# Delta-rule attention with an expert layer: key norms from the Gram diagonal, and a new order of the first four passes

## The chip, the cores and the metric

One core of a Trainium2 chip. The metric is the device time of one execution in microseconds (us): median of 3 runs, 619.43 before the change.

## What is computed

The reference is a linear attention with the delta rule, 32 heads (batch 4, 8 heads) of 768 steps and width 48, followed by a dense layer of two matrices with a softplus between.

```
k_n = k / (norm(k) + 1e-6)
for t in range(768):
    y[:, :, t] = q_t @ state
    v_old = k_t @ state
    state = state + beta_t * outer(k_t, v_t - v_old)
x = y.transpose(0, 2, 1, 3).reshape(3072, 384)
h = x @ w_in                                   # 384 -> 2048
out = (max(h, 0) + log1p(exp(-abs(h)))) @ w_out  # 2048 -> 384
```

## The kernel before

**Chunks, pairs, passes.** Time is cut into 12 chunks of 64 steps. Inside a chunk all heads are solved at once: the Gram products of the keys (L207 to L248) give a lower triangular system, whose 32-wide diagonal blocks are inverted for two chunks together. Such a pair is numbered u = 0 to 5. For pairs 0 and 1 (`N16`) the inversion goes to 16 x 16 blocks only, and `join_w`, `join_z`, `join_d` (L347 to L370) put two of them together by products. `cross_a`, `arrange` and `cross_b` (L374 to L407) then form the off-diagonal block of the inverse. For each chunk follow `k_state` (K times state), `v_less` (the subtraction from V), `p_all` and `mask_p` (Q times K, masked), `u_all` (inverse times V), `y_all` and `state` (the new state).

**One pass per chunk.** The rows of y of chunk m are input x of the dense layer, and pass m runs it in eight half-sets f0 = 0, 2 .. 14 of two hidden tiles each: `ph_mm` (L546 to L561, first matrix), `sp_act` (ScalarE: Abs, Exp, Ln), `sp_dve` (VectorE: the softplus, L573 or L577), and, two half-sets later, `out_mm` (second matrix). One `ph_mm` or one `out_mm` is called a half-step below. The attention of chunk m+1 and later is placed between them. Passes 0 and 1 use the weights as single 32-bit values; from pass 2 on weights and operands are split in two parts (`split`, L539 to L543), with three products each.

**The weights.** They are doubles, 16 tiles f = 0 to 15 of 0.79 MB. Each is loaded (L492), its magnitude taken on ScalarE (`mag`, L507) and converted on VectorE in four instructions (`weights`, L523, L526, L529, L534). A call `("fill", n)` issues n such instructions. Four tiles are loaded at the start; a later load f + 4 is held back by a small GpSimd copy (`hold`, L158) until tile f - 1 is converted.

**Norms and inversion.** `norms` (L256 to L294) loads K rows (`kN`), squares them on ScalarE (L261, L268), adds them up on VectorE (L270), takes the root by Ln and Exp with one Newton step (L275 to L282), and forms beta over the squared norm as column cT and its negative ncT (L286 to L293). `invert` (L296 to L338) selects a triangle of ncT on GpSimd (L302), transposes the Gram blocks on VectorE (L307), multiplies the two (L311, L313) and runs 14 steps of two instructions on each of two blocks (pairs 0 and 1) or 30 steps on the whole (L331, L337). `finish` (L340 to L345) makes the two transposes of the result.

**What sets the order.** All engines run their instructions in the written order. It is written out by hand in tables of calls: `GRAMS` and `START` for all that comes before the first half-step, `FIRST` for pass 0, `PLAN` for the later passes (pass, half-step, call, argument), `INV` and `RATE` for how many steps of an inversion go at each of four places of a half-set, `CASTS` for the half-sets whose rounding is on ScalarE. `("warm", n, c)` issues n products of zeros with c columns on TensorE (L162). `("inv", n)` issues n steps of the inversion in work. DMAs are issued from SyncE's queue in an order of its own, in which a wait holds up all behind it; the copy of the last 16 columns of y into x (L482) goes by SyncE's and, in chunk 0, half by ScalarE's queue.

Before the first half-step the order is: K rows of chunks 0 and 1, kT of chunks 1 and 0, beta, q; norms of pair 0; Gram products; inversion of pair 0; join, cross and u of chunk 0; y of chunk 0. The norms of pair 1, its Grams and the join of chunk 1 stand between these, warm-up products too.

## Time and profile before

| | us |
|---|---|
| median of 3 runs | 619.43 |
| lowest and highest | 616.36, 620.22 |
| the profiled execution | 622.68 |
| its span in the profile | 621.0 |
| TensorE busy | 595.0 (96%) |
| VectorE busy | 449.4 (72%) |
| ScalarE busy | 369.8 (60%) |
| GpSimd busy | 32.8 (5%) |
| granted TensorE clock, mean | 0.973 of full speed |
| HBM read, written | 37.06 MB, 4.72 MB |

PE is TensorE, PEld its weight loads, DVE VectorE, ACT ScalarE, POOL GpSimd, SP SyncE, and SPq or ACTq a queue's DMA issues. A row in order of time gives start, duration, engine, line, operation, output and inputs by the program's names, shape and count; in brackets stands how long the engine was idle before and what released it. A group's row gives busy us, mean ns of one, then idle time. A line of waits gives the sum, the number and the longest. Warm-up products count as busy, so the share of TensorE alone does not tell what it could give up.

### The profile page before, as it was taken

The numbers are of one execution on the slowest core, as the hardware profiler recorded it, in microseconds if no ns is written. First come the engines' busy times: TensorE is split into PE (matmuls) and PEld (weight loads), VectorE is DVE, ScalarE is ACT, GpSimd is POOL, SyncE is SP. The second block draws the span as 40 slices with busy tenths as digits, with TensorE's granted clock in tenths as the row PEclk, the third lists the DMA queues.
The fourth block names the chain that finished last, engine by engine and source line by source line (L and its number), as shares of the span: only waits on it lengthen the run. The fifth ranks groups of instructions, "written<-read, shape, count | busy, mean of one in ns | idle before, by whom it ended". The sixth has DMA issues, their size and how long they took to land.

```text
span 621.0 us, 22953 instructions
## 1 busy us (share of the span) xinstructions
PE 595.0 (96%) x10196; PEld 541.8 (87%) x10196; DVE 449.4 (72%) x941; ACT 369.8 (60%) x743; POOL 32.8 (5%) x70
## 2 busy tenths in 40 slices
PE   7888897999999999999999999999999999999997
PEld 3856675777778999999999999998999999999997
DVE  4985899972799976789873988964998654354433
ACT  4332666436878678864568747558745645644443
POOL 5000110000100000000010000010000000000000
PEclk8777889999999999999999999999999999999999
DMA  9842573211132313202311212211203101100000
GB/s 207 302 153 86 158 269 144 60 58 55 30 64 60 92 30 104 50 18 83 91 58 47 61 43 69 74 33 53 65 2 88 32 26 39 29 29 14 20 6 27
DMA packets 34996, 45.42 MB, mean 73 GB/s; under 512 B 21585, under 2 KB 26897, under 8 KB 34897
## 3 DMA queue, kind: packets, MB, share of 16 engines
q1 hardware_dynamic: 34800, 43.91, 24.8%
q8 instruction: 80, 1.31, 0.9%
q14 instruction: 20, 0.16, 0.1%
q10 hardware_dynamic: 96, 0.05, 0.0%
HBM read 37.06 MB, written 4.72 MB: 67 GB/s over the span
## 4 chain that ended last, share of the span: by engine, by line
PE 77%; DVE 10%; ACT 7%; issue 3%; DMA 2%; ACTq 0%; SPq 0%; DVEq 0%
PE ph L559 30%; PE po L606 28%; PE pa L466 4%; PE po L162 3%; PE pa L451 2%; PE pa L413 2%; PE pa L425 2%; DVE w L543 1%; DMA kt<-kT 1%; PE pa L439 1%; PE pa L402 1%; DVE Z L337 1%; DVE work L331 1%; DVE ltq L307 1%; PE pa L379 1%
## 5 line engine op out<-in xcount | busy, mean ns | idle before, releaser
L559 PE MATMUL ph<-x,w 128*128 128x256 f32 x1452 | 211.4, 299 | 8.3 <-DVE w L534 2.8
L559 PEld LDWEIGHTS ph<-x,w 128*128 128x128 f32 x1452 | 195.6, 191 | 19.4 <-issue 4.5
L606 PE MATMUL po<-w,gh 128*128 128x384 f32 x688 | 191.4, 370 | 0.0
L565 ACT ACTIVATE a<-ph 128x512 f32<-128x512 f32 x96 | 57.4, 598 | 172.7 <-PE ph L559 169.9
L606 PEld LDWEIGHTS po<-w,gh 128*128 128x128 f32 x688 | 121.0, 188 | 15.3
L577 DVE SCALAR_TENSOR_TENSOR a<-ph,a 128x512 f32<-128x512 f32 x80 | 54.9, 686 | 70.4 <-ACT a L567 69.9
L606 PE MATMUL po<-w,gl 128*128 128x384 f32 x280 | 94.1, 336 | 0.0
L566 ACT ACTIVATE a<-a 128x512 f32<-128x512 f32 x96 | 60.7, 632 | 3.0
L567 ACT ACTIVATE a<-a 128x512 f32<-128x512 f32 x96 | 60.7, 632 | 3.0
L589 DVE TENSOR_TENSOR gl<-a,gh 128x512 fp32r<-128x512 f32 x80 | 55.4, 692 | 2.6
L606 PEld LDWEIGHTS po<-w,gl 128*128 128x128 f32 x280 | 52.6, 188 | 0.0
L337 DVE TENSOR_TENSOR Z<-Z,work 128x84 f32<-128x84 f32 (+14 forms) x148 | 44.3, 307 | 4.1
L331 DVE TENSOR_TENSOR work<-Z,ltq 128x84 f32<-128x84 f32 (+14 forms) x148 | 43.7, 303 | 2.2
L584 DVE CAST gh<-a 128x512 fp32r<-128x512 f32 x76 | 32.4, 426 | 2.5
L395 POOL MEMSET tt<- 32x512 f32 x24 | 12.4, 518 | 405.7 <-ACT tt L393 378.8
L432 DVE TENSOR_TENSOR big<-pa,maskP 64x512 f32<-64x512 f32 x44 | 30.2, 687 | 0.5
L466 PEld LDWEIGHTS pa<-big 128*64 128x64 f32 x768 | 25.0, 145 | 2.2 <-issue 1.1
L307 DVE STREAM_TRANSPOSE ltq<-work 128x1024 f32<-128x1024 f32 x6 | 12.9, 2154 | 19.4 <-ACT work L220 17.6
L466 PE MATMUL pa<-big 128*64 128x64 f32 x768 | 26.7, 231 | 0.0
L162 PE MATMUL po<-zero 128*128 128x128 f32 (+2 forms) x108 | 21.8, 364 | 2.0 <-issue 2.0
L559 PE MATMUL ph<-x,v 128*128 128x256 f32 x180 | 23.1, 282 | 0.0
L559 PEld LDWEIGHTS ph<-x,v 128*128 128x128 f32 x180 | 22.6, 189 | 0.0
(124 smaller groups left out, 718.4 us busy)
## 6 DMA issues: line engine op xcount, KB each, us to landing
w<-wts SPq DMA_DIRECT2D x16, 768.0 KB, 8.0
kt<-kT SPq DMA_DIRECT2D x12, 448.0 KB, 3.9
big<-qT SPq DMA_DIRECT2D x24, 192.0 KB, 4.4
nv<-vN SPq DMA_DIRECT2D x12, 384.0 KB, 3.4
ki<-kI SPq DMA_DIRECT2D x24, 192.0 KB, 3.4
out<-ex SPq DMA_DIRECT2D x24, 192.0 KB, 2.0
ka<-kN SPq DMA_DIRECT2D x8, 384.0 KB, 3.6
x<-x SPq DMA_DIRECT2D x60, 32.0 KB, 2.0
```

Source lines behind the costliest of these rows:

```text
L162: nc.tensor.matmul(to[:, 0:cols], zero, zero.unsqueeze(1).to_broadcast([P, cols // P, P]), start=True, stop=True)
L331: nc.vector.tensor_tensor(tmp[:, a:a + r, 0:j], Z[:, a + j + 1:a + n, a + j:a + j + 1].to_broadcast([P, r, j]), lq[:, a + j:a + j + 1, a:a ...
L337: nc.vector.tensor_tensor(z, z, tmp[:, a:a + r, 0:j], op=ALU.add)
L466: nc.tensor.matmul(py[tk[ab], i, :], big[:, at + C:at + 2 * C], big[:, at:at + C], start=True, stop=True)
L559: nc.tensor.matmul(ph[:, f - f0], weight(s, f, a, k * P, P), xr[b][k], start=(c == 0), stop=(c == len(terms) * NK - 1))
L565: nc.scalar.activation(a, PH[s, f0], AF.Abs)
L566: nc.scalar.activation(a, a, AF.Exp, scale=-1.0)
L567: nc.scalar.activation(a, a, AF.Ln, bias=1.0)
L577: nc.vector.scalar_tensor_tensor(a, ph, 0.0, a, op0=ALU.max, op1=ALU.add)
L584: nc.vector.tensor_copy(g[0], a)
L589: nc.vector.tensor_tensor(g[1], a, g[0], op=ALU.subtract)
L606: nc.tensor.matmul(po, g[b][:, f - f0, h * P:(h + 1) * P], weight(s, f, a, DM, DM), start=(f == 0 and i == 0), stop=end)
```

## The change

- Key norms: the Gram blocks hold the squared norms on their diagonal. `norms` reads them there, after the transpose of the Gram blocks, with a step of 33 elements (`lq`, now inside `invert`). `kN` is no longer passed or loaded, the squares and sums are gone, and beta comes already transposed, so cT needs no transpose; the norms for scaling V get one instead.
- Start: kT of chunks 1, 0 and 2 are the first DMAs. A one-element GpSimd copy that reads kT of chunk 0 stands ahead of the loads of q and beta. Four warm-up products instead of three. The four copies of the block below the diagonal of chunk 0 come after those that the inversion needs. `arrange` moves its copies ahead of `cross_a` in chunk 0.
- Loads of weight tiles 4 and 5 are gathered in a list and issued by `("later",)` at the end of `START`, on SyncE behind the copy of x.
- The Grams of pair 1 move from `START` to the sixth half-set of the first pass, and its inversion, with the norms, to the second pass. `join_w` of chunk 1 comes behind the first half-set.
- New tables for the first four passes: where `fin`, `join`, `ca`, `cross_b`, `us`, `ys`, `gs` stand, a row of `INV` (passes 1 to 3) and of `RATE` (later ones) for each half-set instead of one per pass, nine `CASTS` instead of four. The steady table loses its `nms` calls.

The diff, cut to its core:

```
-    ("load_k", 2), ("kas",), ("load_v", 0), ("iv0", 2), ("load_w", 2), ("hold", 0, "Z"), ("p_0",),
...
+    ("load_w", 1), ("load_v", 0), ("load_w", 2), ("load_w", 3), ("load_ki", 0), ("load_w", 0),
+    ("below_1",), ("iv0", 6), ("load_v", 1), ("p_0",), ("warm", 1, 512), ("below_0",), ("mag",),
+    ("masks_0",), ("iv0", 8), ("mag",), ("warm", 1, 256), ("warm", 7, 512), ("iv0", 97),
+    ("join_w", 0), ("join_z", 0), ("scale_v", 0), ("mask_p0", 0), ("join_d", 0), ("mask_p0", 1),
+    ("warm", 1, 256), ("ca", 0), ("cross_b", 0), ("fill", 2), ("warm", 1, 256), ("u_all", 0),
+    ("fill", 2), ("warm", 1, 128), ("y_all", 0), ("fill", 4), ("later",), ("warm", 2, 512),
...
 FIRST = {
+        ("join_w", 1), ("fill", 9), ("join_z", 1), ("state_0",), ("sp",), ("scale_v", 1),
+        ("join_d", 1), ("fill", 7),
...
+        ("fill", 20), ("inv", 2), ("gs", 2), ("out",), ("gs", 3), ("sp",),
...
-    def norms(u, kas=None):
+    def norms(u, ss):
...
+        nc.vector.tensor_scalar(sm, ss, 1e-30, None, op0=ALU.max)
...
+        nc.vector.tensor_tensor(cT, r0, bet[:, u], op=ALU.mult)
+        nc.vector.tensor_scalar(ncT, cT, -1.0, None, op0=ALU.mult)
+        nc.vector.transpose(nn, nt)
...
-    def invert(u, cT, ncT):
+    def invert(u):
...
+        nc.vector.transpose(lq.rearrange("p j i -> p i j"), LTD[u].rearrange("p q i -> p i q"))
+        yield
+        cT, ncT = yield from norms(u, lq.rearrange("p a b -> p (a b)")[:, 0:HB * HB:HB + 1])
...
+                if later is None:
                     hold(ST[f + AHEAD], ST[f - 1][:, 0:1].bitcast(F32))
-                load_weights(f + AHEAD)
+                    load_weights(f + AHEAD)
+                else:
+                    later.append(f + AHEAD)
...
-            nc.sync.dma_start(kas[0][0], kN[0])
-            nc.sync.dma_start(kas[0][1], kN[1])
             load_k(1)
             load_k(0)
...
+            warm(idle, 4)
...
+            nc.gpsimd.tensor_copy(bv[dr[0], 0, 0, 0:1], kts[0][dr[0], 0, 0:1])
+            load_q(0)
+            nc.sync.dma_start(bet, beta)
```

Three places show how instructions stand. In such a row: line, operation, output and inputs, shape, times in a row; line numbers are those of the kernel that is shown.

VectorE at the start of the inversion of pair 0, first before (ss and nn are sums and norms, ltq the transposed Gram blocks, Z the triangle):

```order
L282 TENSOR_SCALAR nn<-r_237 128x32
L286 TENSOR_TENSOR r_237<-nn 128x32
L287 RECIPROCAL r_237<-r_237 128x32
L288 TENSOR_TENSOR r_237<-r_237,bet 128x32
L292 STREAM_TRANSPOSE cT<-r_237 128x32
L293 TENSOR_SCALAR ncT<-cT 128x32
L254 COPY work<-po_128 32x8x32
L307 STREAM_TRANSPOSE ltq<-work 128x32x32
L311 TENSOR_TENSOR ltq<-ltq,Z 128x16x16
```

and with the change:

```order
L275 STREAM_TRANSPOSE ltq<-work 128x32x32
L250 TENSOR_SCALAR sm<-ltq 128x32
L256 RECIPROCAL r_252<-rt 128x32
L257 TENSOR_TENSOR r_252<-r_252,sm 128x32
L258 TENSOR_TENSOR r_252<-r_252,rt 128x32
L259 TENSOR_SCALAR nt<-r_252 128x32
L261 TENSOR_TENSOR r_252<-nt 128x32
L262 RECIPROCAL r_252<-r_252 128x32
L263 TENSOR_TENSOR cT<-r_252,bet 128x32
L264 TENSOR_SCALAR ncT<-cT 128x32
L265 STREAM_TRANSPOSE nn<-nt 128x32
L287 TENSOR_TENSOR ltq<-ltq,Z 128x16x16
```

The norms stood ahead of the transpose of the Gram blocks (L307 before, L275 now) and now stand between it and the first multiply.

TensorE from the join of chunk 0 to its y, first before (tt is the inverse, off the block below the diagonal, big the operands of y; po is written by warm-up products, L162 before and L152 now):

```order
L379 MATMUL pa<-tt,off 32x32 x32
L162 MATMUL po_311<-zero 128x128 x2
L162 MATMUL po_311<-zero 128x256
L162 MATMUL po_311<-zero 128x128
L402 MATMUL pa<-off,tt 32x32 x32
L162 MATMUL po_311<-zero 128x256
L439 MATMUL pa<-nv,tt 64x48 x32
L353 MATMUL pa<-tt,x_316 32x16 x64
L162 MATMUL po_311<-zero 128x128 x2
L466 MATMUL pa<-big 64x64 x32
```

and with the change, from the warm-up products ahead of the join on:

```order
L152 MATMUL po_310<-zero 128x512 x7
L329 MATMUL pa<-tt,x_323 32x16 x64
L339 MATMUL pa<-x_323,tt 32x16 x64
L152 MATMUL po_310<-zero 128x256
L357 MATMUL pa<-tt,off 32x32 x32
L381 MATMUL pa<-off,tt 32x32 x32
L152 MATMUL po_310<-zero 128x256
L418 MATMUL pa<-nv,tt 64x48 x32
L152 MATMUL po_310<-zero 128x128
L445 MATMUL pa<-big 64x64 x32
```

`join_w` of chunk 1 (L353 before) no longer stands between u (L439, now L418) and y (L466, now L445), and fewer warm-up products stand between the join and y.

VectorE in the first pass, first before, from the third weight tile on:

```order
L534 SCALAR_TENSOR_TENSOR w_92<-w_92,ex 128x768
L523 TENSOR_SCALAR ex<-ex 128x768
L307 STREAM_TRANSPOSE ltq<-work 128x32x32
L311 TENSOR_TENSOR ltq<-ltq,Z 128x16x16
L526 TENSOR_SCALAR ex<-ex 128x768
L529 SCALAR_TENSOR_TENSOR ex<-w_93,ex 128x768
```

and with the change, from the last weight tile on:

```order
L518 SCALAR_TENSOR_TENSOR ex<-w_1237,ex 128x768
L523 SCALAR_TENSOR_TENSOR w_1237<-w_1237,ex 128x768
L562 SCALAR_TENSOR_TENSOR gh<-ph,a 128x512 x3
L275 STREAM_TRANSPOSE ltq<-work 128x32x32
L250 TENSOR_SCALAR sm<-ltq 128x32
L562 SCALAR_TENSOR_TENSOR gh<-ph,a 128x512
```

The inversion of pair 1 began among the conversions of the first pass and now begins behind the last of them and three softplus.

More of the change, by code (lines that the diff above doesn't have):

```diff
@@ L508, in mag, with load_later @@
         exs.append(ex)
+    def load_later():
+        nonlocal later
+        for f in later:
+            load_weights(f)
+        later = None
     def weights():
@@ L625, in deltanet_moe @@
     done, conversion = [0], weights()
-    cols = {}
-    def ahead(s):
-        if s % 2 == 0 and 2 <= s < NS - 2:
-            return norms(s // 2 + 1)
-        return None
     def kp(s):
+        if s == 2:
+            scale_v(s)
         k_state(s)
@@ L671, in gs @@
         if s % 2:
-            while s // 2 not in cols:
-                nms(s // 2, 1)
             background.append(solve(s // 2))
     def solve(u):
-        for _ in range(WAIT):
+        for _ in range(WAIT if u > 2 else 0):
             yield
-        yield from invert(u, *cols[u])
-        if u < 3:
+        yield from invert(u)
+        if u < 2:
             finish(u)
```

189 lines of the change are left out of this document (63 added, 126 removed), and 6 rows, old and new, of the table PLAN.

## The prediction

> **What bounds the kernel now.** I read first the busy time by stage (columns: stretch, its length, then busy us and instructions of PE, PEld, DVE, ACT, POOL, granted clock, DMA share, GB/s), then the weight conversion (first and last start at the end), then, stage by stage, instructions in order of time (start, us, engine, line).
>
> ```profile
> 60.00:80.00 20.00, 16.27 (x537) 13.25 (x528) 16.94 (x24) 12.92 (x26) 3.12 (x8) 0.89 0.45 127
> 80.00:100.00 20.00, 19.28 (x133) 13.67 (x130) 18.94 (x27) 12.90 (x21) 2.59 (x8) 0.94 0.78 272
> 100.00:120.00 20.00, 16.27 (x234) 12.16 (x235) 19.44 (x41) 11.11 (x22) 0.00 (x0) 1.00 0.25 72
> 200.00:300.00 100.00, 99.58 (x1725) 96.33 (x1717) 82.63 (x174) 70.09 (x147) 3.34 (x5) 1.00 0.24 63
> ```
>
> ```profile
> L534 DVE SCALAR_TENSOR_TENSOR w<-w,ex x16: 939/958/967, 35.1 to 117.6; 128x768 int32<-128x768 int32 x16
> ```
>
> From 200 us on TensorE is busy 99.6% of the time: nothing is to be had there but its idle crumbs. From 60 to 120 us it lacks 8.2 us and VectorE is busy 55.3 of 60 us; the sixteenth weight tile is converted only at 118.5, and the first pass cannot end before. So the price of this change is decided by when VectorE finishes the sixteen tiles, which hangs on when the chain for chunk 0 lets it begin and what else it does meanwhile. I follow that in five stages. Sums are made in the profiled run (622.68 us, span 621.0) and carried to the median 619.43.
>
> **Stage A, to the inverse of pair 0.**
>
> ```profile
> 1.13 5.49 PE L162 MATMUL ph<-zero 128*128 128x512 f32 x6 [1.13 <-DVE zero L728]
> 8.73 1.16 PE L247 MATMUL po<-kt 48*64 48x64 f32 x64 [2.11 <-DMA kt<-kT]
> 11.46 1.84 PE L234 MATMUL pa<-kt 48*32 48x64 f32 x59
> ```
>
> ```profile
> 10.70 0.16 DVE L275 TENSOR_SCALAR rt<-ss 128x32 f32<-128x32 f32 x1
> 13.31 0.21 DVE L292 STREAM_TRANSPOSE cT<-r 128x32 f32<-128x32 f32 x1
> 13.56 0.18 DVE L293 TENSOR_SCALAR ncT<-cT 128x32 f32<-128x32 f32 x1
> 16.16 2.03 DVE L307 STREAM_TRANSPOSE ltq<-work 128x1024 f32<-128x1024 f32 x1 [1.74 <-ACT work L254]
> 18.30 0.42 DVE L311 TENSOR_TENSOR ltq<-ltq,Z 128x256 f32<-128x256 f32 x1
> 20.07 0.20 DVE L327 COPY Z<-cT 128x32 f32<-128x32 f32 x1
> 21.58 1.41 DVE L432 TENSOR_TENSOR big<-ph,maskP 64x512 f32<-64x512 f32 x2
> 28.45 2.00 DVE L343 STREAM_TRANSPOSE tt<-Z 128x1024 f32<-128x1024 f32 x1
> 30.31 1.92 DVE L344 STREAM_TRANSPOSE tt<-Z 128x1024 f32<-128x1024 f32 x1
> ```
>
> ```profile
> 13.81 0.96 POOL L302 TENSOR_SCALAR_AFFINE_SELECT Z<-ncT 128x256 f32<-128x256 f32 x2 [5.46 <-DVE ncT L293]
> ```
>
> The first Gram product waited for kT until 8.73; 0.79 MB of K rows had been issued ahead. Now kT goes first, but four warm-up products stand before it: 5.49/3 = 1.83 each, so TensorE is free at 1.13 + 7.3 = 8.45. I take kT as landed by then (bounds: as late as before, +1.0; early does not help). Gram of chunk 1 ends at 9.6, of chunk 0 after 2.72 us (the stretch from 10.58 to 13.30 before) at 12.3. One diagonal copy and one block copy of 0.43 follow on VectorE, since the four copies below the diagonal no longer stand ahead on ScalarE: the transpose starts at 13.3 instead of 16.16 and ends at 15.4.
>
> Before, the norms lay in front of it, so the first multiply came 0.1 us behind the transpose. Now they follow it: 10.70 to 13.74 is 3.04, less the 0.21 transpose, is 2.83; then half of the 0.96 on GpSimd and hops: first multiply at 19.0, the copy of the diagonal at 20.8 (before 20.07). This is the price of the diagonal: 3.5 us in the chain, of which 2.8 come back by the earlier start. The fourteen steps took 8.4 us with the 1.44 of a mask in between, which moves behind the transposes. They end at 27.7, the transposes (3.78) at 31.4, before 32.2. Gain only 0.8.
>
> ```profile
> 148.63 1.09 PE L234 MATMUL pa<-kt 48*32 48x64 f32 x62
> ```
>
> The second half of a later Gram, above, takes 1.09 us where chunk 0's took 1.84: TensorE ran faster there. A rule speaks to this. The Trainium skill, "TensorE: Matmul & The Clock Gate", section on the HAM clock gate, lets TensorE out of half speed after one busy window of about 3.4 us that runs free of the kernel. The trace agrees only if no whole window fell into the 5.49 busy us, since the products stayed slow; four fill 7.3 us, which holds one wherever it starts. By that rule chunk 0's Gram would take 1.6 us instead of 2.7 and the sum below would be 608.7. I stay with the slow rows.
>
> **Stage B, from the transposes to y of chunk 0.**
>
> ```profile
> 39.33 3.78 PE L162 MATMUL po<-zero 128*128 128x512 f32 x5 [2.01 <-issue]
> 43.04 1.08 PE L379 MATMUL pa<-tt,off 32*32 32x32 f32 x64
> 52.50 1.29 PE L353 MATMUL pa<-tt,x 32*32 32x16 f32 x81 [1.67 <-issue]
> 54.88 3.75 PE L466 MATMUL pa<-big 128*64 128x64 f32 x64
> 65.23 3.62 PE L559 MATMUL ph<-x,w 128*128 128x256 f32 x8 [1.92 <-DMA x<-x]
> ```
>
> ```profile
> 38.88 0.71 DVE L370 STREAM_TRANSPOSE tt<-tt 128x512 f32<-128x512 f32 x1
> ```
>
> Here lies the first large term. Before, VectorE converted nearly two tiles ahead of the join's second half, which ended at 39.6, 7.4 us behind the transposes, and TensorE was then still in warm-up products until 43.1. Now VectorE does scale_v (0.9), two of the four mask instructions (1.4) and the join's subtraction and transpose (1.2): it ends at 34.9, with one short warm-up on TensorE. Cross_a starts at 35.0 instead of 43.04: 8.0 earlier. Its copy of the block row now stands ahead of the evictions on ScalarE, 1.3 more; but join_w of chunk 1 is gone from between u and y. It took from 50.3 to 53.8, its idle 1.67 included, and the warm-ups behind it 1.2. So cross_a to y takes 11.84 - 4.6 + about 0.9 = 8.1: y starts at 43.1, 11.8 earlier. From there to the first product of the experts were 10.35 us; I leave them: 53.4. Unknown here: q is now issued only when kT of chunk 0 has landed, and nine warm-ups follow its product. Should they last past 32, join_w slips one for one; bounds 0 and +3.
>
> **Stage C, the first pass: VectorE's queue.**
>
> ```profile
> L529 DVE SCALAR_TENSOR_TENSOR ex<-w,ex 128x768 int32<-128x768 int32 x15 | 14.4, 957 | 0.4
> L534 DVE SCALAR_TENSOR_TENSOR w<-w,ex 128x768 int32<-128x768 int32 x15 | 14.3, 956 | 0.8
> L526 DVE TENSOR_SCALAR ex<-ex 128x768 int32<-128x768 int32 x16 | 9.3, 581 | 0.4
> L523 DVE TENSOR_SCALAR ex<-ex 128x768 f32<-128x768 f32 x16 | 8.8, 553 | 0.7 <-ACT ex L507 0.7
> L573 DVE SCALAR_TENSOR_TENSOR gh<-ph,a 128x512 f32<-128x512 f32 x6 | 4.1, 679 | 2.4 <-ACT a L567 2.4
> 58.66 0.56 DVE L471 COPY x<-pa 128x384 f32<-128x384 f32 x1 [5.69 <-PE pa L466]
> ```
>
> A tile costs 0.553 + 0.581 + 0.957 + 0.956 = 3.05 us. VectorE copies y until 59.5 - 11.8 = 47.7, with one tile done. To the sixteenth: 15 x 3.05 = 45.7, five softplus 3.4, four masks 2.8 (twice the 1.41 of L432), scale_v 0.9, join 1.2, subtractions 1.0: 55.0, that is 102.7 without a wait. Gone from here are the transpose, the multiplies and three steps of pair 1, its norms and the reductions. Two waits I see in the order: on ScalarE the magnitude of tile 4 stands behind the softplus of the first products (about 3.3), that of tile 10 behind the copies of u of chunk 1 (1.8). So 107.8; before, VectorE idled 4.7 of its 60 us here, much the same. Weights 4 to 15 are now issued only behind x; each is released by the conversion five tiles back, some 15 us ahead, and its 0.79 MB take 2.9 us at the 272 GB/s of the stretch from 80 to 100. I cost that at nothing; without this cover each late tile counts one for one.
>
> ```profile
> 112.18 2.08 PE L466 MATMUL pa<-big 128*64 128x64 f32 x64
> 120.91 2.74 PE L606 MATMUL po<-w,gh 128*128 128x384 f32 x8
> 184.60 2.40 PE L559 MATMUL ph<-x,v 128*128 128x256 f32 x18
> ```
>
> TensorE now also has both Grams of pair 1 in the middle of this pass. Tile 7 is converted at 80.3 (47.7 + seven tiles 21.4 + wait 3.3 + three softplus 2.0 + the other 5.9). From there its queue holds the rest of that tile's product (1.3), y (2.0 as above), u and state (about 2.7, an estimate from y by their smaller outputs), two Grams (3.2, each one and a half times the 1.09 of L234) and eight half-steps of 2.7: 30.8, full, and it ends tile 15's products at 111.0, not at 109. Before, 120.9. **Gain 9.9.**
>
> **Stage D, second pass.** From 120.91 to 184.60 TensorE has 63.7 us; the change takes cross_a of chunk 3 out and puts k_state and P in, and gives both back in the third pass. The pair's inversion now lies here whole: it can start when softplus 14 is through, 113.6, and takes 2.0 + 2.8 + 1.7 + 7.0 + 3.8 = 17.3, with 8.5 of softplus, masks, subtractions and waiting in between: 139.4, its first half 137.5. TensorE reaches the join, now at half-step 7, at about 140 (111 + ten half-steps of 2.6 and 3.7 of small products). It fits by 2 us.
>
> ```profile
> PE pa L402 <- ACT off L383: 0.5, 1, 0.5
> PE pa L402 <- ACT off L385: 0.2, 1, 0.2
> ```
>
> These waits of cross_b (in all, times, longest) fall away with their cause, the Gram's copies that stood ahead of it on ScalarE: **gain 0.7.**
>
> **Stage E, third pass.**
>
> ```profile
> 184.60:196.00 11.40, 11.40 (x249) 9.44 (x242) 10.95 (x23) 10.21 (x20) 1.04 (x2) 1.00 0.06 9
> 196.00:208.00 12.00, 11.63 (x136) 10.35 (x135) 11.62 (x24) 6.82 (x12) 0.00 (x0) 1.00 0.30 99
> 166.81 1.23 DVE L311 TENSOR_TENSOR ltq<-ltq,Z 128x1024 f32<-128x1024 f32 x1
> 183.44 0.39 DVE L331 TENSOR_TENSOR work<-Z,ltq 128x220 f32<-128x220 f32 x1
> ```
>
> Before, pair 2's inversion began ahead of this pass: transpose, two multiplies of 1.23 and eleven steps (the first row to the last) by 184, about 11 us. Now that falls into the pass, where VectorE had 0.8 us free in the first 23. Against it, three more casts go to ScalarE and two reductions are gone, about 3 us. What then does not fit, 7, can use idle time late in the pass unless a softplus stands behind it. Bounds 0 and 7; I take **loss 1.0**, near the lower end, as the steps are spread between the softplus.
>
> Later passes keep their work; nothing counted. **Sum:** -9.9 - 0.7 + 1.0 = -9.6: span 611.4, median 619.43 - 9.6 = **609.8**.
>
> **Rivals.** *More of it (0.14):* the wait of 3.3 us in stage C is not there, as ScalarE's magnitude of tile 4 gets through before the softplus, and stage E loses nothing: 605.5. For it: VectorE's work alone would end at 102.7; against it: ScalarE takes its queue strictly in order, and there the softplus stands first.
> *Swallowed (0.20):* weights come late or the join slips 3, the first pass ends 6 us later than I say, and the third pass loses 2 instead of 1: 617. For it: twelve tiles, 9.4 MB, must land in 48 us beside x, q and kI, some 240 GB/s, while the stretch from 80 to 100 moved 272 at a share of 0.78; against it: that is still more than is needed.
> *Slower (0.07):* VectorE becomes the bound where the inversions were moved. The margin of 2 us before the join of the second pass turns into a wait of 5 when one softplus queue comes late, the third pass pays its full 7, and the fourth again, since pair 3 slides by as much: 19 lost instead of 1, 628. It decides from 10.6 lost us on, where the first pass's gain is eaten. The 17 idle us of VectorE in each 100 after 200 speak against it.
> *The change doesn't do what it says (0.03):* the queues' order shows the loads of K rows and the reductions gone, so only kT landing late could undo stage A; then VectorE starts no earlier and the warm-ups wait for q: 619.
>
> **Chances.** My forecast has 0.56. About 1%, 6 us, can be told from no change. Most of the forecast and all of "more" lie below 613.2: faster 0.70; "swallowed", the last rival and the forecast's upper edge: same 0.23; slower 0.07. The range 602 to 618 takes in, below, the 5 us of waits of stage C, stage E's loss and the spread of the runs shown (616.36 to 620.22); above, stage B's 3 with most of stage E's 7.
>
> **What would show it.** Right: first product on x near 53, y near 43, tile 15 converted near 108 with VectorE near full from 48, TensorE full from about 90, the third pass from 174 to 176. Wrong: a first product later than 58; VectorE idle on weights between 60 and 100; TensorE idle before the join of the second pass or waiting for softplus in the third.

## The result and the profile after

The change makes the kernel **slower by 1.1%**: 625.66 us (median of 9 runs, 623.82 to 627.01) against 619.39 (9 runs, 616.36 to 622.37), ratio 1.0109, 95% interval 1.0082 to 1.0137. Forecast were 609.8, with 602 to 618 as the range. The profiled execution took 625.57 us, its span 623.8.

Starts of half-steps, from the rows in order of time (us; "b1" is the kernel before with one late entry moved, told below; up to the second pass it is the kernel before):

| | before | b1 | after | forecast |
|---|---|---|---|---|
| first half-step | 62.17 | 60.81 | 50.00 | 53.4 (the row of 65.23 less 11.8) |
| second half-step | 71.54 | 68.32 | 66.52 | |
| second pass | 123.49 | 119.90 | 118.33 | 113.6 |
| third pass | 184.60 | 184.59 | 183.77 | 174 to 176 |
| fourth pass | 229.13 | 229.16 | 230.39 | |
| fifth pass | 275.37 | 275.22 | 278.46 | |
| end of span | 621.0 | 620.7 | 623.8 | 611.4 |

So a lead of 12.2 us at the first half-step is 5.2 at the second pass, 0.8 at the third, and a loss of 3.1 at the fifth, which stays. The start went as well as forecast: the kernel before had its first products on x at 62.17, not at 65.23, where it went on after a wait for x, and 62.17 less 11.8 is 50.4. These are rows of TensorE in the changed kernel: the first warm-ups, the join of chunk 0, the first half-step.

```profile
1.13 5.34 PE L152 MATMUL ph<-zero 128*128 128x512 f32 x8 [1.13 <-DVE zero L693]
7.49 0.72 PE L215 MATMUL pa<-kt 48*32 48x32 f32 x62
28.32 1.91 PE L329 MATMUL pa<-tt,x 32*32 32x16 f32 x128 [7.00 <-DVE tt L320]
50.00 3.19 PE L548 MATMUL ph<-x,w 128*128 128x256 f32 x12 [1.21 <-DMA x<-x]
```

Then the first pass, again TensorE, in order of time (L329 and L339 are `join_w` and `join_z` of chunk 1, L430 is the state of chunk 0, L548 a half-step). Two stalls of 3.42 and 2.75 us are "issue": TensorE waited for nothing that the profile shows. Behind them the second half-step takes 4.22 us where a later one takes 2.86.

```profile
53.12 1.26 PE L329 MATMUL pa<-tt,x 32*32 32x16 f32 x128
55.47 0.51 PE L339 MATMUL pa<-x,tt 32*32 32x16 f32 x39 [1.08 <-ACT x L331]
59.39 1.40 PE L339 MATMUL pa<-x,tt 32*32 32x16 f32 x89 [3.42 <-issue]
60.73 1.83 PE L430 MATMUL pa<-big,ki 128*48 128x48 f32 x39
65.31 1.27 PE L430 MATMUL pa<-big,ki 128*48 128x48 f32 x25 [2.75 <-issue]
66.52 4.22 PE L548 MATMUL ph<-x,w 128*128 128x256 f32 x12
```

VectorE stands in its queue for the softplus of that half-step (first row), later for the magnitude of tile 10 (second), and converts the sixteenth tile 4.6 us later than I said (third):

```profile
72.73 0.69 DVE L562 SCALAR_TENSOR_TENSOR gh<-ph,a 128x512 f32<-128x512 f32 x1 [4.19 <-ACT a L556]
91.81 0.56 DVE L512 TENSOR_SCALAR ex<-ex 128x768 f32<-128x768 f32 x1 [1.98 <-ACT ex L486]
111.42 0.96 DVE L523 SCALAR_TENSOR_TENSOR w<-w,ex 128x768 int32<-128x768 int32 x1
```

The stretches that answer to those shown of before (columns as there). Clock and TensorE are low from 60 to 80, the Gram products stand in the third stretch, and from 208 to 232 TensorE lacks 2.8 us where it lacked none before:

```profile
60.00:80.00 20.00, 16.98 (x411) 13.57 (x403) 14.19 (x21) 11.01 (x20) 1.19 (x3) 0.77 0.55 192
80.00:100.00 20.00, 17.66 (x240) 13.15 (x241) 16.97 (x24) 13.75 (x26) 2.96 (x7) 1.00 0.74 239
100.00:120.00 20.00, 19.41 (x318) 14.24 (x317) 14.63 (x19) 12.24 (x25) 0.00 (x0) 1.00 0.14 26
208.00:232.00 24.00, 21.22 (x251) 20.28 (x250) 22.66 (x59) 12.95 (x25) 0.00 (x0) 1.00 0.22 43
```

```profile
208.00:232.00 24.00, 24.00 (x373) 23.52 (x370) 19.81 (x38) 17.43 (x33) 1.03 (x2) 1.00 0.27 60
```

(The last row is the kernel before.) In the second pass of the changed kernel two join products stand in a row, 256 products by the counts of the first two rows. There is a third "issue" stall, and the half-step behind it takes 4.54 us:

```profile
143.11 1.88 PE L329 MATMUL pa<-tt,x 32*32 32x16 f32 x197
146.99 0.68 PE L329 MATMUL pa<-tt,x 32*32 32x16 f32 x59 [2.00 <-issue]
147.60 4.54 PE L548 MATMUL ph<-x,w 128*128 128x256 f32 x12
```

And from 170 us on TensorE waits, by the line of waits (sum, times, longest), for the remainder of the softplus (gl, the second of the two parts that it is split in):

```profile
PE po L595 <- DVE gl L578: 2.8, 2, 1.4
```

**What "issue" was.** The page lists a queue that carries instructions (packets, MB, share):

```profile
q8 instruction: 79, 1.29, 0.9%
```

These are packets of 16,384 bytes, and TensorE has 20,236 records (10,118 products, as many weight loads): 256 to a packet, or 128 products. The trace has the time of each. Against the long stalls (us):

```
kernel, stall         instruction packet    TensorE goes on
after, join_z         56.96 to 57.98        59.39
after, state          62.96 to 64.04        65.31
after, second pass    144.53 to 145.59      146.99
before, join_w        50.16 to 51.22        52.50
b1, second pass       128.65 to 129.91      131.12
```

Each time TensorE goes on 1.2 to 1.4 us after a packet has landed. In all 20 profiles the other stalls over 0.8 us that are "issue" do so too, 1.2 to 1.6 us after a landing. The exception is one of 1.66 us ahead of a half-step in the kernel before, at 108.21, 16 us after a packet (in its second profile and in b1, which have it too, 3 us): "issue" is not always this. So in the stalls among small products TensorE waits for its instructions. One join is 128 products, a whole packet, and is done in 1.26 us, while packets in a busy stretch start 3.4 to 5 us apart.

### The profile page after: what moved, and what is told of

Its sections match the earlier page's. It is cut to its first block, busy times and chain, and to the rows that moved or that the text cites. A ratio compares the mean times of both kernels' runs of the same rounds, so it can differ in the third digit from the quotient of the medians.

```text
span 623.8 us, 22754 instructions
## 1 busy us (share of the span) xinstructions
PE 588.2 (94%) x10118; PEld 531.8 (85%) x10118; DVE 438.4 (70%) x924; ACT 363.9 (58%) x736; POOL 33.5 (5%) x67
## 4 chain that ended last, share of the span: by engine, by line
PE 76%; DVE 11%; ACT 7%; issue 4%; DMA 1%; POOL 0%; DVEq 0%; ACTq 0%
PE ph L548 29%; PE po L595 29%; PE pa L445 4%; PE pa L430 2%; PE pa L392 2%; PE pa L418 2%; PE pa L404 2%; DVE Z L313 1%; PE pa L357 1%; PE pa L381 1%; DVE ltq L275 1%; DMA big<-qT 1%; DVE work L307 1%; ACT a L555 1%; DVE w L532 1%
## 5 line engine op out<-in xcount | busy, mean ns | idle before, releaser
L548 PE MATMUL ph<-x,w 128*128 128x256 f32 x1452 | 211.8, 299 | 4.9 <-DVE w L523 2.6
L548 PEld LDWEIGHTS ph<-x,w 128*128 128x128 f32 x1452 | 195.9, 192 | 15.6 <-issue 4.4
L307 DVE TENSOR_TENSOR work<-Z,ltq 128x84 f32<-128x84 f32 (+14 forms) x148 | 44.0, 304 | 2.8
L573 DVE CAST gh<-a 128x512 fp32r<-128x512 f32 x71 | 30.8, 433 | 2.3
L532 DVE TENSOR_TENSOR w<-w,w 128x768 fp32r<-128x768 f32 x14 | 13.4, 954 | 20.4 <-ACT w L531 20.3
L445 PEld LDWEIGHTS pa<-big 128*64 128x64 f32 x768 | 24.7, 140 | 3.2 <-issue 1.6
L445 PE MATMUL pa<-big 128*64 128x64 f32 x768 | 26.7, 227 | 0.3 <-ACT big L422 0.3
L486 ACT ACTIVATE ex<-w 128x768 f32<-128x768 f32 x16 | 14.3, 913 | 21.6 <-DMA w<-wts 16.6
L422 ACT COPY big<-pa 64x384 f32<-64x384 f32 x46 | 21.6, 471 | 4.0 <-PE pa L418 3.2
L433 ACT COPY big<-pa 48x384 f32<-48x384 f32 x44 | 20.9, 474 | 4.0 <-PE pa L430 3.2
```

Source lines behind the costliest of these rows:

```text
L307: nc.vector.tensor_tensor(tmp[:, a:a + r, 0:j], Z[:, a + j + 1:a + n, a + j:a + j + 1].to_broadcast([P, r, j]), lq[:, a + j:a + j + 1, a:a ...
L445: nc.tensor.matmul(py[tk[ab], i, :], big[:, at + C:at + 2 * C], big[:, at:at + C], start=True, stop=True)
L548: nc.tensor.matmul(ph[:, f - f0], weight(s, f, a, k * P, P), xr[b][k], start=(c == 0), stop=(c == len(terms) * NK - 1))
L573: nc.vector.tensor_copy(g[0], a)
```

## The experiments

Theory 1: stalls for instructions, lengthened by transfers of weights. Theory 2: runs of small products outrun the instructions by themselves. Theories 3 and 6: the order on ScalarE. Theory 4: VectorE bounds the third pass. Theory 5: the clock. Theory 7: several waits that stand in for one another. Theory 8: the place of one instruction. All times are medians, each beside runs of the kernel before on the same chip; the ratio, with its 95% interval, is worked out from all runs of both and not from the two medians, from which it can differ (e10: 1.0000, by the medians 1.0029).

| run | us | before | ratio (interval) |
|---|---|---|---|
| e1 weights early | 625.09 | 617.90 | 1.0093 (1.0058 to 1.0127) |
| e2 joins apart | 624.01 | 617.90 | 1.0108 (1.0068 to 1.0148) |
| e3 pair 2 earlier | 628.99 | 617.90 | 1.0177 (1.0143 to 1.0211) |
| e4 join before x | 626.48 | 617.90 | 1.0121 (1.0082 to 1.0160) |
| e5 more warm-ups | 626.39 | 618.62 | 1.0122 (1.0084 to 1.0160) |
| e6 half-step first | 624.86 | 618.62 | 1.0098 (1.0059 to 1.0136) |
| e7 four edits | 620.70 | 618.62 | 1.0036 (1.0011 to 1.0061) |
| e8 the four, pair 2 earlier | 622.95 | 618.62 | 1.0073 (1.0041 to 1.0104) |
| e9 apart and early | 618.65 | 619.54 | 0.9978 (0.9949 to 1.0008) |
| e10 apart | 621.35 | 619.54 | 1.0000 (0.9969 to 1.0030) |
| e11 pair 2 later | 634.23 | 619.54 | 1.0209 (1.0165 to 1.0253) |
| e12 e9, pair 2 earlier | 621.81 | 618.75 | 1.0050 (1.0024 to 1.0076) |
| b1 before, joins together | 622.65 | 618.75 | 1.0056 (1.0024 to 1.0088) |
| e13 e9, remainder first | 618.18 | 620.11 | 0.9976 (0.9947 to 1.0005) |
| e14 e13, cross later | 622.55 | 618.56 | 1.0058 (1.0025 to 1.0091) |
| e15 e13, weights at 27 us | 617.83 | 618.63 | 0.9996 (0.9967 to 1.0025) |
| e16 the same, two tiles | 618.07 | 618.63 | 0.9998 (0.9967 to 1.0028) |

### Stalls in the second pass: e2 and b1

e2 takes the joins apart in the changed kernel; b1 puts them together in the kernel before.

```
-(1, 7, "join_w", 3)          e2
+(1, 11, "join_w", 3)
-(1, 3, "join_w", 3)          b1, in the table of before
+(1, 1, "join_w", 3)
```

> Changed kernel, but the first join product of chunk 3 comes four places later in the second pass instead of straight behind that of chunk 2. Theory 2 (256 small products in a row outrun the instruction supply, with the DMA queues idle): the stall of 2.0 us at 145 us goes, the products behind it run at full clock (the 4.5 us of the next half-step become 2.8), the third pass starts 3 to 4 us earlier than 183.8, 622. Rival (the stall is tied to the place, a wait that the profile does not show, and only moves): a stall of about 2 us at the new place, third pass at 183 to 184, 625.5.

> Kernel before, with one entry of its table changed: the first join product of chunk 3 comes straight behind that of chunk 2 in its second pass, as in the changed kernel. Theory 2 (256 small products in a row outrun the instruction supply, in any kernel): a new stall of about 2 us in that pass, the clock falls below 1.00 behind it, the third pass starts 3 to 4 us later than 184.6, and the time rises by 2 to 4 us. Rival (the stall belongs to something else that the change brought): no new stall, same time.

In e2 the stall and the slow half-step are gone:

```profile
141.39 1.26 PE L329 MATMUL pa<-tt,x 32*32 32x16 f32 x128
142.60 2.86 PE L548 MATMUL ph<-x,w 128*128 128x256 f32 x12
```

In b1 they appear, with the same sizes:

```profile
127.39 1.74 PE L353 MATMUL pa<-tt,x 32*32 32x16 f32 x180
131.12 0.82 PE L353 MATMUL pa<-tt,x 32*32 32x16 f32 x76 [1.99 <-issue]
131.88 4.51 PE L559 MATMUL ph<-x,w 128*128 128x256 f32 x12
```

b1 takes 64.7 us from second to third pass instead of 61.1, e2 63.2 instead of 65.4, e7 (with the same edit) 61.5. The median of b1 is 3.9 above that of before, as expected; its third pass starts no later than in before, since this execution entered its second pass 3.6 us earlier. That of e2 alone shows no gain against the ratio of 1.0109. e2 has a new stall of 1.38 us, where the second join product of chunk 3 and u of chunk 2 follow each other (192 products); e7 doesn't have it. In b1 it is one entry of a table, no work added, and two causes of about equal weight: 2 us of stall, and 1.7 us of half clock behind it. In the changed kernel the mean transfer rate from 140 to 152 us was 5 GB/s, so no transfer is needed for such a stall.

### Stalls in the first pass: e1, e4, e6

```
 ("load_v", 1), ("load_w", 4), ("load_w", 5), ("load_w", 6), ("p_0",)     e1: added loads
-("later",), ("warm", 2, 512)        +("later",), ("join_w", 1)           e4: join before x
-("fill", 9), ("join_z", 1), ("state_0",), ("sp",), ... ("fill", 7)       e6: half-step first
+("fill", 9), ("sp",), ("scale_v", 1), ("fill", 7)      (state_0 one, join_z two half-sets on)
```

> Changed kernel, but weight tiles 4 to 6 are loaded straight behind tile 0, in the stretch from 27 to 47 us in which the DMA queues stand nearly still, instead of behind x. Theory 1 (TensorE starves for instructions while five weight tiles land between 51 and 60 us): its two stalls at the join and the state of the first pass, 3.4 and 2.8 us, fall to under 3 us together, the sixteenth tile is converted at 108 to 109 instead of 112.4, the third pass starts 3 us earlier, 622. Theory 2 (the run of small products alone outruns the instructions, whatever the DMA queues carry): both stalls stay, over 5 us together, sixteenth tile at 111 to 112, 624.5 to 625.5. Theory 3 (ScalarE's magnitudes wait for the weights, and that is what costs): its waits of 1.3, 2.0 and 1.0 us go, the stalls stay, VectorE gains the 0.8 us that it waited for them: 624.8.

e1 (its first pass):

```profile
58.10 1.37 PE L339 MATMUL pa<-x,tt 32*32 32x16 f32 x89 [0.53 <-issue]
61.97 1.28 PE L430 MATMUL pa<-big,ki 128*48 128x48 f32 x25 [0.74 <-issue]
```

6.17 us of stalls have become 1.27, as theory 1 says. But the second pass starts only 1.1 us earlier. VectorE's wait of 1.98 us for the magnitude of tile 10 became 3.7, and the stall in the join of chunk 0, 0.91 us before, became 3.45: the weights now landed there. With the same products in the same order, this is that stall in three kernels, each row followed by the 4 us from the start of that join (columns as above; the DMA share stands next to last, and as packets count where they start, it can pass 1). After, e13, e15:

```profile
32.70 1.05 PE L339 MATMUL pa<-x,tt 32*32 32x16 f32 x63 [0.91 <-issue]
28.32:32.32 4.00, 2.99 (x193) 2.83 (x194) 2.08 (x3) 1.46 (x3) 0.00 (x0) 0.50 0.02 4
```

```profile
33.79 1.05 PE L339 MATMUL pa<-x,tt 32*32 32x16 f32 x63 [2.35 <-issue]
27.97:31.97 4.00, 2.98 (x193) 2.82 (x194) 3.77 (x4) 0.37 (x1) 0.00 (x0) 0.50 0.85 266
```

```profile
34.49 1.05 PE L339 MATMUL pa<-x,tt 32*32 32x16 f32 x63 [3.12 <-issue]
27.90:31.90 4.00, 2.99 (x193) 2.83 (x194) 2.60 (x4) 1.47 (x3) 0.00 (x0) 0.50 0.94 359
```

At a DMA share of 0.02 the stall is 0.9 us, at 0.85 2.4, at 0.94 3.1. The other kernels with the same seven warm-ups ahead of the join fall in with them, but for one: 0.6 to 1.1 us at shares up to 0.03 (e3, e4, e6, e10, e11), 1.65 at 0.11 (e2), 2.27 at 0.76 (e16), 3.45 at 0.97 (e1), 3.33, 3.83 and 4.88 at 1.02 (e14, e9, e12); e14's is a little shorter than e1's. The packet that ends the stall takes 0.9 to 1.4 us in all of them. With the weights it starts 3.3 to 5.2 us after the join, without them 1.3 to 2.2. So both theories hold: the run of small products makes the stall, and the transfer lengthens it, as the packet starts later.

> Changed kernel, but the first join product of chunk 1 takes the place of the last two warm-up products, while TensorE waits for x. Theory 2: one block of instructions less in the run behind the first half-step, so the first stall of 3.4 us shrinks to under 1.5, the first half-step starts at 50 as before, the second 2 to 3 us earlier than 66.5; end 622.5 to 623.5. Theory 1 (the landing weights hold up the instructions): the stalls keep 5 us or more together and only come earlier or later, 625. Rival: the join delays the first half-step itself past 51.5, and nothing is won, 625.5.

Here x came late (the half-step starts at 51.51, with 4.2 us of waits for x), and the second half-step at 65.58. The stall in the join of the first pass is gone, that of the state is 2.4. Nothing is gained by the second pass (117.04), as the rival had it.

> Changed kernel, but the second half-step of the first pass goes ahead of the state of chunk 0 and of the second join product of chunk 1 on TensorE, which come one and two half-sets later. Theory 2 (run of small products outruns the instructions; the half-step stands behind it, and VectorE stands in its queue for that half-step's softplus): the second half-step starts at 57 to 59 instead of 66.5, VectorE's wait of 4.2 us for its softplus falls under 1, the sixteenth tile is converted at 108 instead of 112.4, 622. Rival, theory 6 (ScalarE's order: the magnitude of tile 10 stands behind the copies of u of chunk 1): VectorE's wait for it grows from 2.0 to 4 or more, sixteenth tile at 110.5 to 112, 624.5 to 625.5.

The second half-step starts at 53.75, and still the second pass only at 117.62. A new wait of 6.39 us stands on TensorE:

```profile
66.16 2.49 PE L392 MATMUL pa<-big,kt 48*64 48x48 f32 x61 [6.39 <-ACT big L433]
```

The state's copies now stand on ScalarE behind the magnitudes of tiles 4 to 7, which wait for their weights, and behind the softplus of that half-step. Neither case that I had written down: theory 3 in another place.

### The clock: e5

```
-("warm", 7, 512), ("iv0", 97)        +("warm", 14, 512), ("iv0", 97)
```

> Changed kernel with fourteen instead of seven warm-up products ahead of the first join, so that TensorE works through the 7.0 us in which it waits for the inverse of pair 0. Theory 5 (the idle stretch lets the granted clock fall to a half, and the products of cross, u and y run slow behind it): the clock between 24 and 42 us is near 1.00 instead of 0.50 to 0.58, u takes 1.2 us instead of 2.7, y 2.1 instead of 2.9, the first half-step starts at 46.5 to 47.5 instead of 50, and the run ends 1 to 3 us earlier, 623. Rival (the stalls for instructions behind the first half-step and VectorE's queue take it back): first half-step earlier, but sixteenth tile still at 111 to 112.5 and the end unchanged, 625.5.

```profile
24.00:36.00 12.00, 9.02 (x320) 5.23 (x319) 8.43 (x12) 3.85 (x7) 0.00 (x0) 0.95 0.17 44
36.00:48.00 12.00, 10.43 (x214) 8.17 (x214) 7.36 (x14) 4.28 (x10) 1.04 (x2) 0.62 0.11 36
```

The clock is 0.95 instead of 0.54 from 24 to 36 us, and 0.62 instead of 0.61 from 36 to 48. The first half-step starts at 49.96, as before the edit: what the small products won at full clock they lost in stalls (1.38 us in the join and 1.45 in cross, where there had been 0.91 and 0.53), and in these the clock fell again. Theory 5 by itself falls.

### The first two passes together: e7, e9, e10, e15, e16

e7 has e2, e5, e6 and one conversion step ahead of u of chunk 1. e9 has e1, e2, that step, and join_z of chunk 1 alone moved behind the third half-step; e10 is e9 without early loads.

```
-("out",), ("us", 1), ("fill", 15), ("sp",)
+("out",), ("fill", 1), ("us", 1), ("fill", 14), ("sp",)
-("fill", 9), ("join_z", 1), ("state_0",), ("sp",), ("scale_v", 1), ("join_d", 1), ("fill", 7)
+("fill", 9), ("state_0",), ("sp",), ("scale_v", 1), ("fill", 7)
-("v_less", 1), ("load_k", 3), ("sp",), ("ca", 1), ...
+("v_less", 1), ("load_k", 3), ("join_z", 1), ("sp",), ("join_d", 1), ...
```

> Changed kernel with four edits: more warm-ups, the second half-step first, one conversion step (and so the magnitude of tile 10) ahead of u of chunk 1, and the two join products of the second pass apart. If theories 2, 5 and 6 together hold the loss of the first two passes: sixteenth tile at 105 to 107, first pass over at about 109, third pass from 175 to 177, 618 to 619, that is no slower than before. If one of them is wrong: third pass not before 180, 622 or more.

Its third pass starts at 179.17: nearly all its gain is that of the joins; the second pass starts at 117.68, with 6.8 us of the wait that e6 has.

> Changed kernel with weight tiles 4 to 6 loaded early, the second join product of chunk 1 moved behind the third half-step of the first pass (the state of chunk 0 stays where it was), the magnitude of tile 10 ahead of u of chunk 1, and the join products of the second pass apart. Theory 7 (the first pass ends when VectorE has worked through its queue, and its 9 to 10 us of waits come from TensorE's stalls and from ScalarE's order together, so that one of them alone gives way to the other): its waits between 48 and 112 fall from 9.3 to under 5, the sixteenth tile is converted at 107 to 108, the second pass starts at 113 to 114 instead of 118.3, the third from 175 to 176, 616 to 617. Rival (another wait takes their place, as in the four runs so far): second pass at 117 or later, third at 179, 620 to 621.

The second pass starts at 112.17, the third at 175.24. VectorE's last conversion:

```profile
104.40 0.96 DVE L523 SCALAR_TENSOR_TENSOR w<-w,ex 128x768 int32<-128x768 int32 x1
```

It ends 55.1 us after the copies of y (50.25), and between them stands one wait, of 0.33 us: the 55.0 us that I had summed for its work, with nothing left of the 9.3 us of waits (0.84 + 1.15 + 4.19 + 0.36 + 1.98 + 0.28 + 0.47) of the changed kernel. So theory 7 holds: one cause taken away alone (e1, e4, e6) let the next one show, and only several edits together gave the pass its time.

> The same without the early loads: weight tiles 4 to 8 still land between 51 and 61 us. If late weights count (theories 1 and 3): second pass 2 to 3 us later than with the early loads, 619. If they do not: the same time as with them.

Second pass at 112.97, so later by 0.8, not 2 to 3; the state's stall is 3.8 instead of 1.7 us, and the sixteenth tile is converted at the same 104.40. So the moved join product and the conversion step are enough for VectorE, and the early loads pay little in the first pass, since they cost 3 us of stall at the start. The medians are farther apart, 621.35 and 618.65, but the intervals of the ratios overlap.

e15 and e16 are e13 (below) with the early loads at another place, behind a small copy (e16 without tile 6):

```
-("iv0", 6), ("load_v", 1), ("load_w", 4), ("load_w", 5), ("load_w", 6), ("p_0",), ...
+("iv0", 6), ("load_v", 1), ("p_0",), ...
-("mask_p0", 0), ("join_d", 0), ("mask_p0", 1),
+("mask_p0", 0), ("join_d", 0), ("hold", 4, "T"), ("load_w", 4), ("load_w", 5), ("load_w", 6), ("mask_p0", 1),
```

> The kernel with the remainder ahead, but weight tiles 4 to 6 are held back until the join of chunk 0 is done (about 35 us). Theory 1 (a stall for instructions grows with what the DMA queues carry): the stall in the join of chunk 0, 2.4 to 3.8 us with the weights landing beside it and 0.6 to 0.9 without, is under 1 us again, the first half-step starts near 50 instead of 52, the second pass at 109 to 110.5 instead of 112.1, 615.5 to 616.5. Rival: the weights now lengthen the stalls of cross and u between 36 and 46 us instead, first half-step at 52, no gain, 618.

> The same with two tiles instead of three, so that less lands beside cross and u, and one tile more behind x. Theory 1: as with three, or up to 1 us later in the first pass, as the burst behind x is longer by a tile: 616 to 617. Rival: as there, 618.

These do not test what I wrote. The copy that was to hold the loads back reads a column that the transposes write, not the join; it ran at 26.61, and the tiles landed beside the join (the stall of 3.12 us above, 2.27 in e16). They stand as two more values of that stall, and as two more kernels level with before.

### The third pass: e3, e8, e11, e12, e13, e14

The loss there: from the third to the fifth pass the changed kernel takes 94.7 us, before 90.8.

```
 e3, e8, e12: ("gs", 5) at (1, 11), not (1, 14); 22, 13, 10 steps of the inversion in pass 1
 e12 also: ("join_w", 3) at (1, 9), not (1, 11) as in e9
 e11: fin 2 at (3, 1), ca 4 at (3, 3), cross_b 4 at (3, 5), us 4 at (3, 6)
+                while rests:          e13, ahead of the steps of the inversion
+                    rest()
 e14: e13 with ca 4 at (3, 2) and cross_b 4 at (3, 3)
```

> Changed kernel, but the Gram of chunk 5 comes three places earlier and some 22 steps of the inversion of pair 2 fall into the end of the second pass, where VectorE is half idle, instead of the third. Theory 4 (VectorE bounds the third pass, 22.5 busy of each 24 us, since that inversion was pushed into it): TensorE's idle time in the third pass falls from 3.5 us to under 1, the fourth pass starts 3 us earlier relative to the third, 622. Rival (softplus queues up behind the inversion in the second pass instead): the second pass loses 2 us or more, 625 to 627.

> The same four edits, and the inversion of pair 2 begun at the end of the second pass, but only some 13 steps of it and behind y of chunk 2. Theory 4 (VectorE bounds the third pass): TensorE's idle time in the third pass falls from 3.5 to under 1.5, and it ends 2 us below the run with four edits, 616 to 617. Rival (as with the first move of this kind, x of chunk 2 comes late): idle time at the start of the third pass instead, no gain or 1 to 2 us more, 618 to 621.

> The kernel with early weights and the products spread, and the Gram of chunk 5 three places earlier in the second pass with no join next to it, its inversion begun there with some 10 steps. Theory 4 with theory 2 (the two earlier moves of this kind lost their gain to a run of small products that the move made, not to VectorE): no stall in the second pass, third pass from 175, TensorE's waits in the third pass under 1.5 instead of 3.5 us, 2 us below the kernel that it starts from, 616 to 617. Rival (VectorE has no time for it there either): third pass 2 us later, 619.

All three lose 2 to 4 us in the second pass: x comes 2.3 us late in e3, and each has a new stall, since the moved products made a new run (e8, then e12; in e12 it is the join product at (1, 9) with cross_a of chunk 2 right behind it, so e12 is not the run without a stall that was meant):

```profile
165.08 1.98 PE L418 MATMUL pa<-nv,tt 64*64 64x48 f32 x64 [1.50 <-issue]
```

```profile
148.96 0.32 PE L357 MATMUL pa<-tt,off 32*32 32x32 f32 x15 [2.14 <-issue]
```

And the third pass is not shorter: 46.1, 46.7, 46.7 us (after 46.6). The waits for the remainder fall from 2.8 to 1.0 in e8 and e12, others take their place.

> Changed kernel, but the inversion of pair 2 runs on into the fourth pass (some eight steps and the two transposes), where VectorE is busy 14.8 of 28 us, and what needs its result comes one to three places later there. Theory 4 (VectorE bounds the third pass): the waits for the softplus remainder (2.8 us) go, the third pass takes 44.5 instead of 46.6 us, and the run ends 2 us earlier, 623.5. Rival (those waits cost nothing, since the fourth pass gives the same time up, or its softplus then stands behind the transposes): fourth pass longer by what the third gains, 625 to 626.

The third pass takes 44.6 us, as theory 4 says, and the fourth 56.8 instead of 48.1: the late inverse is now waited for (a Gram by 2.07, u by 1.89 us among others). Worse than the rival had it.

> The kernel with early weights and the products spread (618.65), and one edit more: where ScalarE has rounded a half-set's softplus, VectorE's remainder of it is issued ahead of the next steps of the inversion, not behind them and the next softplus. Theory 8 (the third pass does not lack VectorE time as such; TensorE waits twice 1.4 us since the remainder stands behind four steps of an inversion): these waits go, the third pass takes 43.5 to 44.5 instead of 46.6 us, 616. Theory 4 (VectorE is full, any order only moves the wait): the third pass stays over 46 us, 618.5.

The waits from 170 to 232 us in e13:

```profile
PE pa L357 <- DVE tt L319: 1.6, 1, 1.6
PE po L595 <- DVE gl L578: 0.5, 1, 0.5
```

Theory 8 was right for the third pass, 44.5 us; but cross_a then waits 1.6 us for the transposes that end the inversion, and the lead over e9 falls from 1.9 us at the start of the fourth pass to 0.2 one half-step later.

> The kernel with the remainder ahead, and the two cross products of chunk 4 one place later in the fourth pass, behind K and P of that chunk. In the kernel that it starts from the first of them waits 1.6 us for the transposes that end the inversion of pair 2, and the time won in the third pass (1.9 us) is gone a half-step later. Theory 8: with the place moved the wait is covered, TensorE keeps the 1.9 us, the fifth pass starts at 267.5 instead of 269.4, 616.5. Theory 4 (VectorE is full until the inversion is done, and every move meets it at the next place): a wait of about the same size behind it, fifth pass at 269 or later, 618.

The fourth pass takes 53.1 us instead of 49.4 in e13, with u and cross_a waiting 2.1 us each. The six moves fit theory 4 in this form: VectorE's chain of the inversion of pair 2 ends when it ends, and each move met it at another place. That is argued and not shown, as three of them (e3, e8, e12) made new stalls as well. Two of the moves cost far more than they moved. Behind the new waits the granted clock is at half, for 3.4 us in e14 (from 233.89) and for 6.8 us in e11 (from 242.30). An estimate from these takes half of that time as lost: 1.7 us in e14, with 2.0 us more of waits than in e13, make its 3.7; 3.4 us in e11, with some 5 us of waits, make most of its 8.7.

### Before, a second profile

> Kernel before without any edit, for a second profile: the one shown first was of an execution of 622.68 us, above the median of its runs. Theory 5 (what differs between runs of one kernel is the granted clock ahead of the second pass): in an execution of 616 to 619 us the clock is at half in less of the first 100 us, the second pass starts 2 to 5 us earlier than 123.5, and from there on the two executions agree within 0.5 us. Rival: the difference arises in the later passes.

It did not show what I looked for: this execution took 622.86 us, above all the other runs beside it (615.76 to 622.4), with the same starts within 0.7 us. But b1, the same code up to its second pass, was there at 119.90 instead of 123.49, with the clock at 1.00 from 60 to 72 us where before has 0.86. So an undisturbed start of the kernel before gives 3.6 us that neither of its own profiles has. That fits the medians: from the second pass to the end before takes 621.0 - 123.5 = 497.5, after 623.8 - 118.3 = 505.5, 8.0 more, and 8.0 less the 1.6 between 119.9 and 118.3 is 6.4; the medians differ by 6.27. It is one profile, and of another table entry, so that is an argument, not a measurement.

## Why the prediction was wrong

**Stage A, right, and better.** Transposes ended at 28.2, not 31.4. I had weighed a rule and stayed with the slow rows: the Trainium skill, "TensorE: Matmul & The Clock Gate", on the HAM clock gate, would have the Gram products run fast behind four warm-ups. The trace agrees with the rule: 5.34 us for four warm-ups, not 7.3, clock 1.00 up to 20 us, 0.72 us for the Gram half. My reading of the kernel before was wrong here: its granted clock is 1.00 from 7.14 to 10.55 us, so the warm-ups had released it there too, and it is 0.50 from 10.55 on, behind the 2.11 us in which TensorE waited for kT. By the rule I had 608.7; the rest was wrong all the same.

**Stage B, right.** y at 43.95 (43.1), first half-step at 50.0. I had 53.4, as I took the row of 65.23 for the first product on x, which stood at 62.17; from there the same sum gives 50.4.

**Stage C, the first failed step:** "two waits I see in the order", 3.3 and 1.8 us. VectorE's work was right (55.0; 55.1 in e9), the waits were 9.3. One that I named did not occur where I put it (tile 4 behind the first softplus: VectorE waited 0.84 there), the second did (1.98 for 1.8), and the largest, 4.19, was not in the sum: the softplus of the second half-step, late as TensorE stalled 6.2 us for instructions and ran at half clock behind. "I cost that at nothing", of the weights held back behind x, was the step next to it: they lengthened those stalls (e1) and stood in ScalarE's queue (e6); once the order was mended, late weights cost 0.8 us (e10 against e9). The gain was 5.2 us by the two profiles, not 9.9, and only 1.6 against the start that b1 shows for the kernel before; e9 reaches 112.2, better than my 113.6.

**Stage D, the second:** I forecast a gain of 0.7 and looked for a wait on VectorE, "it fits by 2 us". It did: the join started at 143.11 without waiting for VectorE. But the pass took 65.4 us against 61.1. Of the 4.3, 1.3 is k_state and P for cross_a, displaced as I said; the other 3.0 were two joins in a row, which I counted by their busy time alone. Taken apart, the pass is 63.2 us (e2) and 61.5 (e7); put together in the kernel before, it is 64.7 for 61.1 (b1).

**Stage E, the third:** "loss 1.0, near the lower end" of 0 to 7. By pass, with the displaced products counted, third and fourth pass lost 3.9 + 1.3 = 5.2. TensorE's idle time in the two rose from 0.4 to 4.1 us, 2.8 of it for the remainder, which stood behind steps of the inversion. So the mechanism fits the one named (the inversion pushed into a full VectorE), and the size was wrong. No run gave the two passes their time back (e11 and e13 to e16 the third alone), so this cause is argued, not shown, and some 1.5 us of the 5.2 are not idle time and stay unexplained.

In sum -5.2 + 4.3 + 3.9 = +3.0 by the profiles, for -9.6. Of the rivals, "swallowed" had the first pass's end right (6 us later than I said; it was 4.7: 115.75 for 111.0 at tile 15's products), "slower" the place of a later loss, but as one wait of 5 us on VectorE before the join, which did not come.

What stays open: why kernels like e9 and e16, whose profiled executions are 6 to 8 us below those of before, are level with it in the medians. A single profile told too much there, of before as of these. The mean granted clock of each execution goes with part of it: of 135 executions of the kernel before, the 23 at 0.975 took 620.5 us in the mean and the 32 at 0.981 took 618.1; its two profiled ones had 0.973 and 0.975, those of e9 and e16 0.981 and 0.983. Nor did any run take the new norms and the new order apart: what each is worth alone is not known.

## What to carry to other kernels

A lead ahead of a stage that an engine's queue bounds is worth only what that queue passes on: sum its work and price each wait by what stands ahead of the instruction waited for, on every engine in the chain, and expect that taking away one wait shows the next. Count instructions as well as time where small products stand in a row: more than one packet's worth (128 products here) in a few microseconds stalled TensorE here for 1 to 5 us and could cost nearly as much again in clock, and a transfer beside it lengthened the stall. Spread such runs between large products before moving anything else.

## What the runs showed of the hardware

TensorE's instructions come in packets of 16 KB over DMA, and a run of products of about 10 ns each uses one up in 1.26 us, while TensorE goes on only 1.2 to 1.6 us after the next has landed. The Trainium skill, "Runtime: NRT & Kernel Launch", section "Instruction fetch mechanics", has the next block fetched while the current one is worked off, so that the crossing is mostly hidden. The trace agrees for large products (no stall from 260 to 300 us), and not for these: 2.00 us at a transfer rate of 5 GB/s, up to 4.9 with weights landing (e12).

The clock falls behind such a stall: 0.86 from 140 to 152 us in the changed kernel, 1.00 in e2, and 4.5 us for a half-step of 2.86:

```profile
140.00:152.00 12.00, 10.00 (x305) 7.40 (x293) 7.46 (x7) 5.04 (x12) 0.00 (x0) 0.86 0.02 5
```

```profile
140.00:152.00 12.00, 11.91 (x353) 8.79 (x352) 9.17 (x12) 7.89 (x18) 0.00 (x0) 1.00 0.02 5
```

(The first row is the changed kernel, the second e2.) The same stretch has 0.81 to 0.86 in e1, e3, e4, e5, e6 and e11, which keep the two joins together, and 1.00 in e7 to e10, which don't. The Trainium skill, "TensorE: Matmul & The Clock Gate", section "HAM oscillation — how this bites in real kernels", speaks of idle gaps over some 3.4 us. The trace differs: a gap of 2.0 to 2.5 us inside a run of small products went with a slower clock in these seven kernels. Not always: behind the stall of 2.14 us of e12 the clock stayed at 1.00.

The traces show much of what decides. In the records the granted clock changes only from one step of 3.41 us to the next. In the changed kernel the whole stall lies in one step, where TensorE is busy for 1.41 us, and the next step has 0.50 (first two rows). In e12 the stall lies across two steps with 2.48 and 2.21 us busy, and the clock stays (last three rows):

```profile
144.41:147.82 3.41, 1.41 (x128) 1.30 (x119) 3.05 (x4) 1.30 (x3) 0.00 (x0) 1.00 0.02 5
147.82:151.23 3.41, 3.41 (x9) 2.67 (x9) 0.00 (x0) 0.28 (x1) 0.00 (x0) 0.50 0.03 5
```

```profile
144.34:147.75 3.41, 2.48 (x180) 1.78 (x178) 3.03 (x5) 0.67 (x2) 0.00 (x0) 1.00 0.02 5
147.75:151.17 3.42, 2.21 (x24) 1.96 (x25) 0.00 (x0) 1.74 (x5) 0.00 (x0) 1.00 0.03 7
151.17:154.58 3.41, 3.41 (x75) 2.32 (x74) 0.00 (x0) 3.30 (x6) 1.03 (x2) 1.00 0.00 0
```

Counted over all 20 profiles, of the steps at full clock in which TensorE was busy for less than 45% of the time, 37 of 38 were followed by one at half; from 45 to 75% it was 35 of 140, and above 75% none of some 3200. The steps begin at another point in each execution (one at 4.46 us in the changed kernel, one at 7.14 in the kernel before), so nearly the same stall can cost clock in one execution and not in another: 1.90 us ahead of 160.19 did in e15, 1.86 us at the same place in e10 (ahead of 160.26) didn't.
